# A two-part kernel on one core: the last output block turned, the first load and scan in two, and a new hand-written order

## The chip, the cores and the metric

One core of one Trainium2 chip runs the whole program. The metric is the device time of one execution in microseconds; the kernel before has a median of 391.71 us over three executions (391.2 to 394.22). The engines have names of their own in the rows: PE is TensorE's multiplication and PEld its weight load, DVE is VectorE, ACT is ScalarE, POOL is GpSimd, SP is SyncE (here the engine that issues nearly all transfers).

## The reference

A linear attention with decays (4 batches, 8 heads, 768 steps, head size 48) feeds a small network with a maximum of three products:

```python
for t in range(S):
    cur = einsum('bhd,bhe->bhde', u[None] * kt, vt)
    y[:, :, t] = einsum('bhd,bhde->bhe', rt, state + cur)
    state = wt[:, :, :, None] * state + einsum('bhd,bhe->bhde', kt, vt)
x = y.transpose(0, 2, 1, 3).reshape(3072, 384)
h = maximum(maximum(x @ w1, x @ w2), x @ w3)      # 3072 x 768
out = (h @ w_out).astype(float32)                 # 3072 x 384
```

The weights of the network arrive as 64-bit floats.

## The kernel before

**Attention.** The 768 steps are cut in 6 chunks of 128 for each of 4 batches, 24 pieces k = 0 to 23. A piece's decays `tin[.., 0:517]` hold four blocks of 129 columns with a zero at each block's border, so that one scan serves four pairs of heads. Its steps have one letter each: `b` the backward scan of the decays (line 406), `p` the floor of four end values (415), `q` their reciprocal (418), `f` the forward scan (421), `r` decays times receptance and key (430), `d`, `e` the diagonal (443 on ScalarE, then 460 on TensorE and 463 on VectorE), `X` the scores (489), `M` their mask (496 on VectorE, 500 on ScalarE), `T` a transposition (511, copied by 513), `R`, `U`, `S`, `m`, `Z` the state, `V` and `Y` the values (593 or 614, with a tiny ScalarE copy "touch" between the two at 598 or 620), `E` the result into `x`, `n` the next load (271), `c3` and the like a check on ScalarE (435).

**The network.** Tokens come in 6 halves of 512 (`HT`). For each half 18 groups (`up`, line 175) make the three products for six blocks of 128 hidden units, ScalarE and VectorE take their maximum out of PSUM (158, 160), and `downs` (211) multiplies with `w_out`. Values and weights are split in a high and a low part, three products each; the first four blocks of the first half use plain 32-bit products. For halves 0 to 4 the result is turned (`across`): three tiles of 128 outputs x 512 tokens, 54 products of 512 columns. For the last half it is natural: four tiles of 128 tokens x 384 outputs, 72 products of 384 columns.

**Weights.** They are loaded (`w`, line 329) and turned to 32 bits: `l` on ScalarE (346, 347), `h` and `c` on VectorE (352, 358), `s` and `o` split them (140, 141).

**Order.** Every engine works through its own instructions in the order in which the program is written, and the order is set by hand: `PARTS` is a list of steps through the first two halves (453 of them, about the first 165 us), and after it a loop takes a fixed mix of attention units and groups. `g..` and `G..` are groups of the first and second half, `D..` and `H..` pieces of `downs`, `t` takes one product out of PSUM. `W10` puts ten products of a tile of zeros into TensorE's queue, `warmer(WARM, LEAD)` the first ones and `warmer(0, BACK)` some after the last product.

**The end.** A flag computed on the way tells whether the fast path's assumptions held. Each engine reads it (line 820) and branches (821) over a slow second path. The last two of the four natural tiles stay in PSUM over that branch (`LATE = 2`); behind it ScalarE copies one and VectorE the other, and SyncE stores each (932, 933).

## Time and profile before

| | |
|---|---|
| three executions | 391.2, 391.71, 394.22 us |
| the profiled execution | 391.18 us, of it 389.5 us span |
| PE busy | 381.7 us (98%) |
| DVE busy | 265.9 us (68%) |
| ACT busy | 173.4 us (45%) |
| POOL busy | 85.2 us (22%) |
| TensorE's granted clock, mean | 0.998 of 2.4 GHz |

The span goes from the first to the last instruction; 1.7 us of the execution lie around it. A product's end is modelled in these records, so a busy PE may still be waiting; how fast it really goes is seen from the starts of products that follow each other.

### The profile page before, as it was taken

What the parts mean: (1) busy time and instruction counts of PE and PEld (TensorE: products, weight loads), DVE (VectorE), ACT (ScalarE), POOL (GpSimd) and SP (SyncE); (2) the same over time, 40 slices, a digit from 0 to 9 for tenths busy, and PEclk for the clock granted to TensorE, in tenths of its full rate; (3) what the DMA queues carried; (4) which work ended last, traced back from release to release, by engine and by line L of the source; (5) the groups of instructions that cost most, each with busy time, mean ns of one, the idle gap of its engine ahead of it and who ended that gap; (6) DMA issues with size and microseconds to landing.
All of it is one profiled execution on the core that took longest, in us unless ns stands there. A gap on an engine that the chain in (4) does not pass through costs nothing.

```text
span 389.5 us, 10503 instructions
## 1 busy us (share of the span) xinstructions
PE 381.7 (98%) x4480; PEld 309.3 (79%) x4480; DVE 265.9 (68%) x399; ACT 173.4 (45%) x373; POOL 85.2 (22%) x102
## 2 busy tenths in 40 slices
PE   8899999999999999999999999999999999999995
PEld 4688867766788888888888888888888887878895
DVE  7999999986779975598778567777568431432320
ACT  4688787643544443333444443443443332421210
POOL 3000000221443252144424314333414100000000
PEclk9999999999999999999999999999999999999999
DMA  7993897301823431477243866143951123200002
GB/s 284 403 347 103 284 406 248 112 2 52 272 68 126 147 127 51 136 292 223 68 173 115 275 198 210 61 168 98 307 201 44 42 82 89 94 3 1 0 24 67
DMA packets 23576, 58.44 MB, mean 150 GB/s; under 512 B 2720, under 2 KB 3712, under 8 KB 23520
## 3 DMA queue, kind: packets, MB, share of 16 engines
q1 hardware_dynamic: 20144, 48.58, 36.0%
q10 hardware_dynamic: 3376, 9.09, 7.3%
q8 instruction: 37, 0.61, 0.6%
q14 instruction: 19, 0.16, 0.1%
HBM read 51.87 MB, written 4.72 MB: 145 GB/s over the span
## 4 chain that ended last, share of the span: by engine, by line
PE 86%; DVE 6%; DMA 3%; ACT 2%; issue 2%; SPq 0%; POOL 0%; ACTq 0%; DVEq 0%
PE psm L175 53%; PE psm L211 18%; PE grams L489 3%; PE y L527 3%; PE y L614 3%; DMA w<-in_w_all_dram 2%; PE psm L511 2%; PE grams L542 1%; DVE w L358 1%; PE grams L460 1%; DVE cv L352 1%; PE grams L211 1%; PE y L211 1%; DMA tin<-in_tin_dram 1%; DVE w L141 1%
## 5 line engine op out<-in xcount | busy, mean ns | idle before, releaser
L175 PE MATMUL psm<-x_hi,w 128*128 128x512 f32 x576 | 183.0, 393 | 0.0
L175 PEld LDWEIGHTS psm<-x_hi,w 128*128 128x128 f32 x576 | 108.1, 188 | 23.5 <-issue 0.2
L175 PE MATMUL psm<-x_lo,w 128*128 128x512 f32 x288 | 112.1, 389 | 0.0
L160 DVE TENSOR_TENSOR m<-psm,m 128x512 f32<-128x512 f32 x64 | 43.7, 685 | 51.2 <-PE psm L175 44.2
L175 PEld LDWEIGHTS psm<-x_lo,w 128*128 128x128 f32 x288 | 54.1, 188 | 11.1 <-issue 0.2
L211 PE MATMUL psm<-h_hi,w 128*128 128x512 f32 x180 | 59.5, 430 | 0.3 <-DVE h_hi L160 0.3
L140 ACT CAST h_hi<-m 128x512 fp32r<-128x512 f32 x32 | 19.6, 617 | 54.6 <-DVE m L160 54.6
L211 PEld LDWEIGHTS psm<-h_hi,w 128*128 128x128 f32 x180 | 33.4, 188 | 12.1 <-issue 4.8
L470 POOL TENSOR_SCALAR_AFFINE_SELECT a<-sums 64x512 f32<-64x512 f32 x32 | 25.2, 787 | 72.3 <-DVE sums L467 71.3
L435 ACT ACTIVATE gf<-gf 112x1034 f32<-112x1034 f32 x24 | 25.7, 1070 | 26.4 <-DVE tin L430 26.2
L415 POOL TENSOR_SCALAR d_fwd<-gf 112x4 f32<-112x4 f32 x24 | 6.6, 276 | 134.6 <-DVE gf L406 128.3
L421 DVE TENSOR_TENSOR_SCAN gf<-tin,d_fwd 112x517 f32<-112x517 f32 x24 | 35.6, 1482 | 0.4
L406 DVE TENSOR_TENSOR_SCAN gf<-tin,d_bwd 112x517 f32<-112x517 f32 x24 | 30.2, 1258 | 5.7 <-DMA tin<-in_tin_dram 5.6
L175 PE MATMUL psm<-x,w 128*128 128x256 f32 (+1 forms) x126 | 33.9, 418 | 0.0
L430 DVE TENSOR_TENSOR tin<-tin,gf 112x1024 f32<-112x1024 f32 x24 | 31.1, 1296 | 0.0
L211 PE MATMUL psm<-h_lo,w 128*128 128x512 f32 x78 | 30.4, 390 | 0.0
L141 DVE TENSOR_TENSOR h_lo<-m,h_hi 128x512 fp32r<-128x512 f32 x32 | 23.9, 752 | 7.7 <-ACT h_hi L140 7.5
L175 PEld LDWEIGHTS psm<-x,w 128*128 128x128 f32 x126 | 23.0, 190 | 6.8 <-issue 3.3
L447 POOL TENSOR_TENSOR kr<-kr,u_bc 128x384 f32<-128x384 f32 x16 | 27.7, 1730 | 1.3
L141 DVE TENSOR_TENSOR x_lo<-x,x_hi 128x512 fp32r<-128x512 f32 x18 | 11.4, 685 | 22.7 <-ACT x_hi L140 22.7
L446 POOL TENSOR_TENSOR kr<-kr 128x384 f32<-128x384 f32 x16 | 22.9, 1434 | 9.4 <-DMA kr<-in_nat_dram 8.4
L382 ACT ACTIVATE cv<-cv,mid_top 128x384 f32<-128x384 uint32 x24 | 14.9, 621 | 16.6 <-DVE cv L380 16.5
(99 smaller groups left out, 468.6 us busy)
## 6 DMA issues: line engine op xcount, KB each, us to landing
tin<-in_tin_dram SPq DMA_DIRECT2D x24, 512.0 KB, 4.5
w<-in_w_all_dram SPq DMA_DIRECT2D x25, 384.0 KB, 7.6
w<-in_w_all_dram ACTq DMA_DIRECT2D x23, 384.0 KB, 3.4
v<-in_nat_dram SPq DMA_DIRECT2D x24, 288.0 KB, 5.4
tin<-in_tin_dram SPq DMA_DIRECT2D x24, 262.5 KB, 5.3
kr<-in_nat_dram SPq DMA_DIRECT2D x16, 384.0 KB, 5.1
out_dram<-m SPq DMA_DIRECT2D x15, 256.0 KB, 2.5
x<-x SPq DMA_DIRECT2D x10, 96.0 KB, 2.9
```

What stands on the lines that cost most here:

```text
L140: nc.scalar.copy(out=hi, in_=src)
L141: rest = lambda: nc.vector.tensor_tensor(out=lo, in0=src, in1=hi.bitcast(F32), op=ALU.subtract)
L160: nc.vector.tensor_tensor(out=m[:, cols], in0=ps[:, cols], in1=m[:, cols], op=ALU.max)
L175: nc.tensor.matmul(ps[:, cols], lhsT=wt[i][:, ct * 128:(ct + 1) * 128], rhs=x[part][:, ct, cols], start=(n == 0), stop=(n == KT * len(term ...
L211: nc.tensor.matmul(pss[tt][:, 0:wide_to], lhsT=w[:, cut] if turned else h[:, cut], rhs=h[:, :] if turned else w[:, :], start=(f == 0 and i ...
L406: nc.vector.tensor_tensor_scan(out=g[0:112, ::-1], data0=t[0:112, 0:WC][:, ::-1], data1=d_bwd[0:112, ::-1], initial=0.0, op0=ALU.mult, op1 ...
L421: nc.vector.tensor_tensor_scan(out=prep[k]["f"][0:112, :], data0=tbuf[k % NB][0:112, 0:WC], data1=d_fwd[0:112, :], initial=0.0, op0=ALU.mu ...
L430: nc.vector.tensor_tensor(out=both[0:112], in0=both[0:112], in1=by[0:112], op=ALU.mult)
L435: nc.scalar.activation(out=flat, in_=flat, func=AF.Square, accum_out=acc[0:112, k:k + 1])
L446: nc.gpsimd.tensor_tensor(out=n[:, 0, :], in0=n[:, 0, :], in1=n[:, 1, :], op=ALU.mult)
L447: nc.gpsimd.tensor_tensor(out=n[:, 0, :], in0=n[:, 0, :], in1=u_bc[:, :], op=ALU.mult)
L470: nc.gpsimd.affine_select(out=a[o:o + HC, 0:H, :], in_=cs[o:o + HC, :].unsqueeze(2).broadcast_to([HC, H, HC]), pattern=[[0, H], [1, HC]], ...
```

## The change

The last half is turned as the others: `natural` goes, `downs` has one form, and one tile (`LATE = KT - 1`, 128 x 512) stays in PSUM over the branch. Behind it VectorE copies its first 256 columns and ScalarE the others, and one transfer stores both. The first piece's decays load in two transfers, cut at column 259 (`CUT`), and their backward scan runs as two; their floor moves from GpSimd to VectorE. `PARTS` has the same steps in another order (`W9`, `W4`, `W5` for `W10`, `W3`, `W3`), and three numbers change.

```diff
-WARM = 9
-LEAD = 69
-BACK = 8
+WARM = 8
+LEAD = 86
+BACK = 5
...
-PARTS = """b0 w w p0 q0 f0 d0 b1 e0 p1 q1 R0 w d1 r0 W10 X0 c0 w T0 f1 W3 M0 b2 n3 p2 e1 r1 V0 q2 U0 W3 d2 l w X1 f2 w Y0 E0 M1
+PARTS = """w b0 d0 p0 q0 f0 b1 w R0 e0 p1 q1 W9 r0 w X0 d1 f1 c0 M0 W4 b2 T0 n3 e1 p2 l w W5 q2 r1 d2 f2 V0 X1 c1 M1 T1 h
...
-LATE = 2
+LATE = KT - 1
 LINE = 128
+CUT = NP // 2 * WS + 1
...
         def load(k):
...
-            for cols in (slice(0, WU), slice(RK, TU)):
+            for cols in (*((slice(0, CUT), slice(CUT, WU)) if k == 0 else (slice(0, WU),)), slice(RK, TU)):
                 nc.sync.dma_start(out=t[:, cols], in_=tin[b, c, :, cols])
...
-            nc.vector.tensor_tensor_scan(out=g[0:112, ::-1], data0=t[0:112, 0:WC][:, ::-1],
-                                         data1=d_bwd[0:112, ::-1], initial=0.0, op0=ALU.mult, op1=ALU.add)
+            for cut in (slice(0, CUT), slice(CUT, WC)) if k == 0 else (slice(0, WC),):
+                nc.vector.tensor_tensor_scan(out=g[0:112, cut][:, ::-1], data0=t[0:112, cut][:, ::-1],
+                                             data1=d_bwd[0:112, cut][:, ::-1], initial=0.0, op0=ALU.mult, op1=ALU.add)
...
-            nc.gpsimd.tensor_scalar(out=sep, in0=prep[k]["g"][0:112, 1:WC:WS], scalar1=FLOOR, scalar2=None, op0=ALU.max)
+            eng = nc.gpsimd if k else nc.vector
+            eng.tensor_scalar(out=sep, in0=prep[k]["g"][0:112, 1:WC:WS], scalar1=FLOOR, scalar2=None, op0=ALU.max)
...
-                    nc.tensor.matmul(pss[tt][:, 0:wide_to], lhsT=w[:, cut] if turned else h[:, cut],
-                                     rhs=h[:, :] if turned else w[:, :],
+                    nc.tensor.matmul(pss[tt][:, :], lhsT=wt[FT * 3 + f][:, cut], rhs=ht[f][:, :],
...
-        while groups < GPH * NH - DPH + 2 * CPH:
+        while groups < GPH * NH:
...
-    last = w_p.tile([128, 2, 2 * PC], F32, name=f"w{spot}")
-    for tt in range(LATE, CPH):
-        o = last[:, tt - LATE, 0:PC]
-        (nc.scalar.copy if tt < CPH - 1 else nc.vector.tensor_copy)(out=o, in_=left[tt][:, 0:DM])
-        nc.sync.dma_start(out=natural[tt], in_=o)
+    last = w_p.tile([128, 2, 2 * PC], F32, name=f"w{spot}")[:, 0, 0:HT]
+    nc.vector.tensor_copy(out=last[:, 0:HT // 2], in_=left[:, 0:HT // 2])
+    nc.scalar.copy(out=last[:, HT // 2:], in_=left[:, HT // 2:])
+    nc.sync.dma_start(out=across[NH - 1, LATE], in_=last)
```

The order at three places, first of before and then of the change. SyncE, from the program's first transfer (`tin` decays and keys, `v` and `x` values, `w` weights):

```order
L271 DMA tin_107<-in_tin_dram 128x525
L271 DMA tin_107<-in_tin_dram 128x1024
L271 DMA tin_108<-in_tin_dram 128x525
L271 DMA tin_108<-in_tin_dram 128x1024
L261 DMA v<-in_nat_dram 128x576
L265 DMA x<-in_nat_dram 128x384
L271 DMA tin_109<-in_tin_dram 128x525
L271 DMA tin_109<-in_tin_dram 128x1024
L329 DMA w_242<-in_w_all_dram 128x1536 x2
L261 DMA v<-in_nat_dram 128x576
L265 DMA x<-in_nat_dram 128x384
L329 DMA w_279<-in_w_all_dram 128x1536 x2
```

```order
L268 DMA tin_107<-in_tin_dram 128x259
L268 DMA tin_107<-in_tin_dram 128x266
L268 DMA tin_107<-in_tin_dram 128x1024
L268 DMA tin_108<-in_tin_dram 128x525
L268 DMA tin_108<-in_tin_dram 128x1024
L258 DMA v<-in_nat_dram 128x576
L262 DMA x<-in_nat_dram 128x384
L268 DMA tin_109<-in_tin_dram 128x525
L268 DMA tin_109<-in_tin_dram 128x1024
L326 DMA w_257<-in_w_all_dram 128x1536 x2
L258 DMA v<-in_nat_dram 128x576
L262 DMA x<-in_nat_dram 128x384
```

The first transfer became two, and every later one stands one place further back.

ScalarE, eleven rows from the check of piece 0 (`gf,sums`) on; `kr<-tin_109` is step `d` of piece 2, `cv<-w` and `w<-w` the first weight pair's step `l`, `touch` and `x<-y` belong to the values of the first pieces:

```order
L435 ACTIVATE gf,sums<-gf 112x1034
L513 COPY kn<-psm 128x448
L500 COPY a_137<-grams 128x256
L598 COPY touch<-y 112x2
L443 ACTIVATE kr<-tin_109 112x128 x4
L346 ACTIVATE cv<-w_242,low_end 128x768
L347 ACTIVATE w_242<-w_242 128x768
L632 COPY x<-y 128x3x128
L500 COPY a_138<-grams 128x256
L513 COPY kn<-psm 128x448
L598 COPY touch<-y 112x2
```

```order
L434 ACTIVATE gf,sums<-gf 112x1034
L499 COPY a_138<-grams 128x256
L512 COPY kn<-psm 128x448
L343 ACTIVATE cv<-w_257,low_end 128x768
L344 ACTIVATE w_257<-w_257 128x768
L442 ACTIVATE kr<-tin_109 112x128 x4
L597 COPY touch<-y 112x2
L434 ACTIVATE gf,sums<-gf 112x1034
L499 COPY a_139<-grams 128x256
L512 COPY kn<-psm 128x448
L631 COPY x<-y 128x3x128
```

The first weight pair's two rows moved ahead of the diagonal of piece 2 and of the first `touch`.

The engines behind the branch, with what a row waits for; VectorE's row and then ScalarE's, the last rows of each before the program's end (`PE_49`, `DVE_49` and `Activation_49` are the counts of the three engines' finished instructions, `DMAHW` those of transfers):

```order
L821 UNCONDITIONAL_BRANCH
L821 UNCONDITIONAL_BRANCH [waits DVE_49]
L932 COPY w_6175<-grams 128x384 [waits DVE_49,PE_49]
L997 UNCONDITIONAL_BRANCH
L821 UNCONDITIONAL_BRANCH
L821 UNCONDITIONAL_BRANCH [waits Activation_49]
L932 COPY w_6175<-y 128x384 [waits DMAHW4_49,DVE_49,PE_49]
L997 UNCONDITIONAL_BRANCH
```

```order
L818 UNCONDITIONAL_BRANCH
L818 UNCONDITIONAL_BRANCH [waits DVE_49]
L923 COPY w_5843<-grams 128x256 [waits DVE_49,PE_49]
L989 UNCONDITIONAL_BRANCH
L818 UNCONDITIONAL_BRANCH
L818 UNCONDITIONAL_BRANCH [waits Activation_49]
L924 COPY w_5843<-grams 128x256 [waits DMAHW5_49,DVE_49]
L989 UNCONDITIONAL_BRANCH
```

In ScalarE's row the wait for TensorE's count is gone, and VectorE's count and a transfer's are left; VectorE's row waits for TensorE in both.

## Rows read from the trace of the kernel before

**Rows 1.** Page, parts 1 (busy us, share, instructions) and 4 (chain)
```profile
PE 381.7 (98%) x4480; PEld 309.3 (79%) x4480; DVE 265.9 (68%) x399; ACT 173.4 (45%) x373; POOL 85.2 (22%) x102
...
PE 86%; DVE 6%; DMA 3%; ACT 2%; issue 2%; SPq 0%; POOL 0%; ACTq 0%; DVEq 0%
```

**Rows 2.** Chain of waits: start us, us, what, count; four stretches
```profile
147.81 12.46 PE psm L211 x54
...
372.58 6.26 PE psm L211 x36
...
381.97 3.14 PE grams L211 x18
385.13 0.56 DVE w L932
```

**Rows 3.** Timeline, first 10 us: start, us, engine line operation, count, [idle before <-releaser]
```profile
0.81 1.81 SPq L271 DMA_DIRECT2D tin<-in_tin_dram  x4
...
3.56 1.23 DVE L406 TENSOR_TENSOR_SCAN gf<-tin,d_bwd 112x517 f32<-112x517 f32 x1 [1.11 <-DMA tin<-in_tin_dram]
...
4.88 0.23 POOL L415 TENSOR_SCALAR d_fwd<-gf 112x4 f32<-112x4 f32 x1 [1.24 <-DVE gf L406]
...
5.07 1.28 ACT L443 ACTIVATE kr<-tin 112x128 f32<-112x128 f32 x4 [2.76 <-DMA tin<-in_tin_dram]
...
5.36 1.24 DVE L421 TENSOR_TENSOR_SCAN gf<-tin,d_fwd 112x517 f32<-112x517 f32 x1
...
7.64 0.70 DVE L463 COPY_PREDICATED a<-mask,grams 128x512 f32<-128x512 int32 x1
...
8.31 1.20 DVE L430 TENSOR_TENSOR tin<-tin,gf 112x1024 f32<-112x1024 f32 x1
...
9.56 0.90 PE L489 MATMUL grams<-tin 48*64 48x128 f32 x32 [0.31 <-DVE tin L430]
```

**Rows 4.** Timeline of TensorE, 17 to 22 us
```profile
17.13 0.69 PE L460 MATMUL grams<-tin,kr 48*64 48x64 f32 x32 [0.31 <-ACT a L500]
...
20.55 0.90 PE L489 MATMUL grams<-tin 48*64 48x128 f32 x32
...
21.82 1.47 PE L175 MATMUL psm<-x,w 128*128 128x256 f32 x6
```

**Rows 5.** Timelines of ScalarE and VectorE, a row of each
```profile
14.54 1.02 ACT L346 ACTIVATE cv<-w,low_end 128x768 uint32<-128x768 uint16 x1
...
18.58 1.21 DVE L430 TENSOR_TENSOR tin<-tin,gf 112x1024 f32<-112x1024 f32 x1
```

**Rows 6.** Timeline of TensorE, 72 to 88 us: its two longest waits
```profile
72.23 0.69 PE L460 MATMUL grams<-tin,kr 48*64 48x64 f32 x32 [0.55 <-DVE scur L563]
...
85.66 2.46 PE L211 MATMUL psm<-h_hi,w 128*128 128x512 f32 x6 [0.26 <-DVE h_hi L160]
```

**Rows 7.** Timeline of SyncE's issues after 376 us
```profile
376.84 2.93 SPq L765 DMA_DIRECT2D out_dram<-m  x2
384.07 1.98 SPq L933 DMA_DIRECT2D out_dram<-w  x2
```

**Rows 8.** Timeline of ScalarE after 376 us
```profile
378.94 0.48 ACT L216 COPY m<-psm 128x384 f32<-128x384 f32 x1 [2.12 <-PE psm L211]
382.49 0.48 ACT L932 COPY w<-y 128x384 f32<-128x384 f32 x1 [3.07 <-ACTq L821]
```

**Rows 9.** Groups by form, 0 to 170 us: count | busy us, mean ns
```profile
L160 DVE TENSOR_TENSOR h_hi<-psm,h_hi 128x256 f32<-128x256 f32 x12 | 5.0, 413 | 0.4 <-ACT h_hi L158 0.2 <-PE psm L175 0.2
...
L158 ACT COPY h_hi<-psm 128x256 f32<-128x256 f32 x6 | 2.2, 374 | 1.0 <-PE psm L175 1.0
```

**Rows 10.** Page, part 6: DMA issues, KB each, median us to landing
```profile
out_dram<-m SPq DMA_DIRECT2D x15, 256.0 KB, 2.5
```

**Rows 11.** Line 821, the branch: duration ns min/median/max, first and last start
```profile
L821 SPq EVENT_SEMAPHORE  x8: 17/17/17, 383.3 to 383.9; - x8
...
L821 PEldq COMPARE_BRANCH  x1: 4034/4034/4034, 383.8 to 383.8; - x1
```

More of the change, by code (lines that the diff above doesn't have):

```diff
@@ L142, in split, with moe @@
         rest() if later is None else later.append(rest)
-    def moe(x, pools, store, late=None, plain=0, turned=True):
+    def moe(x, pools, store, late=None, plain=0):
         ps_m, hp, mp = pools
@@ L155, in take_up @@
             m = top[f]
-            n = taken[f, cols.start] = taken.get((f, cols.start), 0) + 1
+            n = taken.get((f, cols.start), 0) + 1
+            for at in range(cols.start, cols.stop, C):
+                assert taken.get((f, at), 0) == n - 1
+                taken[f, at] = n
             if n == 1:
@@ L199, in downs @@
         def downs():
-            order = [(tt, f) for tt in range(KT if turned else CPH) for f in range(FT)]
+            order = [(tt, f) for tt in range(KT) for f in range(FT)]
             order.insert(FT, order.pop(FT - 1))
-            wide_to = HT if turned else DM
             pss = {}
@@ L764, in store @@
             def store(tt, o):
-                nc.sync.dma_start(out=natural[tt] if half == NH - 1 else across[half, tt], in_=o)
-            up, catch_up, ups, down = moe(xs[half], pools, store, late if half == NH - 1 else None, plain=FR if half == 0 else 0,
-                                          turned=half < NH - 1)
+                nc.sync.dma_start(out=across[half, tt], in_=o)
+            up, catch_up, ups, down = moe(xs[half], pools, store, late if half == NH - 1 else None, plain=FR if half == 0 else 0)
             now = dict(half=half, up=up, catch_up=catch_up, ups=ups(), down=down())
@@ L801 @@
         groups = 2 * GPH
-        while groups < GPH * NH - DPH + 2 * CPH:
-            half = min(groups // GPH, NH - 1)
-            g = groups - half * GPH
+        while groups < GPH * NH:
+            half, g = divmod(groups, GPH)
             if g == 0:
@@ L903 @@
         yt = ytr.rearrange("k p b (h t) -> k p b h t", t=C)
-        def again_moe(half, of, turned):
+        with tc.For_i(0, NH) as half:
             x = xs_p.tile([128, KT, HT], F32, name="x")
@@ L914, in store2 @@
             def store2(tt, o):
[L915 to L917 removed]
+                nc.sync.dma_start(out=across[ds(half, 1), tt].rearrange("h p t -> (h p) t"), in_=o)
+            _, _, ups, down = moe(dict(hi=x_hi, lo=x_lo), pools, store2)
             for part in (ups, down):
```

54 lines of the change are left out of this document (21 added, 33 removed).

## The prediction

> **What bounds the kernel now.** First the page's busy times and chain: PE is busy for 381.7 of 389.5 us and makes 86% of the chain [rows 1]. Then, because a busy PE may still be waiting, the stretches of the chain in order of time: 54 products of 512 columns take 12.46 us, 231 ns each, and the last part's 72 products of 384 columns run from 372.58 to 385.11 without a hole (the first 36 and the last 18 stand there), 12.53 us or 174 ns each [rows 2]. From about 20 us on the products follow each other at this pace, so the reader should see two ends and little between them: about 20 us before TensorE has steady work, and 4.4 us behind its last product. Whatever reaches the end must change what TensorE waits for in those first 20 us, its few later waits, or the tail.
>
> The start is a chain of transfer, VectorE, TensorE: the first decays are issued at 0.81, the scan starts at 3.56, GpSimd's floor at 4.88, the forward scan at 5.36, `r` ends at 9.51 and the first scores start at 9.56 [rows 3]. VectorE stands still for almost nothing between 5.36 and 9.51. The first product with weights starts at 21.82, behind the scores of piece 2 at 20.55 [rows 4]. Later the two longest waits of TensorE are 0.55 us at 72.23, for VectorE's state row, and the one ending at 85.66, for a `take_up` of VectorE's [rows 6].
>
> **The change part by part.** I sum against the profiled execution's own 391.18 us; the median of the three, 391.71, lies 0.5 above it.
>
> *The split load and scan, the floor.* Four issues on SyncE take 1.81 us, 0.45 each [rows 3]. The first half's landing has no row. It comes no later than the whole did (scan at 3.56), and with half the bytes I give it 0.3 us, to 3.25; the bound on the other side is 2.9, where a transfer of 2 us or so would put it. A half scan costs between half of 1.23 us and that plus a smallest operation's 0.2: 0.66. The second half is issued 0.45 later and lands inside that time. So the scans end at 4.57, not 4.79. The floor took GpSimd 0.23 us plus two changes of engine, from 4.79 to the reciprocal, which with its own 0.2 leads to 5.36; on VectorE the same four columns cost some 0.1 to 0.2, which saves 0.2. The forward scan starts at 4.95, 0.4 earlier. But the extra issue puts every later transfer back by up to 0.45: the keys of piece 0, for which ScalarE waits until 5.07, land at 5.5, `d` takes 1.28, and TensorE's diagonal and VectorE's copy (7.64) follow it, now at 7.5 [rows 3]. VectorE runs in order, so `r` behind that copy gains only what the copy gains. The first scores start at 9.4, not 9.56. Bounds: 0.6 us gained if the later transfers are held up by nothing but the shared bandwidth, 0.45 lost if they shift whole and the first half lands no sooner.
>
> The Trainium skill's page "VectorE: DVE Perf Modes", section on the TRN2 errata, says that an operation on SBUF pays a fixed latency once per instruction, so that two small ones pay it twice; its 58 to 150 cycles would be an estimated 0.06 to 0.16 us for the second scan. My 0.66 for a half (0.62 is exact half) holds 0.04 of it; by the page the gain here is up to 0.1 us smaller.
>
> *The new order up to the first weight product.* Two things move. VectorE now does `b3`, 1.2 us, before the diagonal and `r` of piece 2; ScalarE does the first weights' `l` before `d2` and the first touch, where before `l` began at 14.54 [rows 5]. `l` cannot start before both weights have landed, and `d2` and the touch are queued behind it; TensorE's `Y0` waits for the touch and its diagonal of piece 2 for `d2`. Before, ScalarE had no idle time ahead of `l` at 14.54, so the weights had landed by then; with 1.9 us for `l` and 1.3 for `d2` the touch comes near 16.2 if they land at 12.9, and TensorE's diagonal of piece 2 at about 17.6, against 17.13 [rows 4]. VectorE's copy and `r2` then end near 20.05, and the scores of piece 2 start at 20.1 against 20.55, because between the two TensorE has only 1.65 us of other work. The first weight product, whose weights VectorE joins behind `r2`, starts at about 21.4 against 21.82. I take **-0.4 us** up to here; the ends are -0.8 and +1.2, the second if the weights land as late as 14.5.
>
> *The order from there to 165 us.* The steps are the same 453, so TensorE's work is the same but for filler in its queue: 26 products of zeros for 25, under the waits of the first 15 us. A shift can come from waits alone. Both long waits of rows 6 lose their cause: the diagonal `e7` now stands 20 steps behind `S6` instead of 9, which releases its accumulator, and the last plain group (`gc3`) no longer stands just ahead of the first piece of `downs` but three groups earlier. The rows show 0.8 us of waiting; as a product's end is modelled late, the true holes are longer, and I count 1.3. A new order has waits of its own that no row shows; with nothing between 0 and as many again plus a slow stretch (+3), I take +1.0. Together **-0.3**, from -1.3 to +1.7. Cover: `r2` ends at 19.79 [rows 5] and its scores start at 20.55, so VectorE may be 0.8 us late there before it is felt.
>
> *The last half.* 54 products at 231 ns are 12.46 us, 72 at 174 ns were 12.53 [rows 2]: **-0.07**. The columns are the same, 27,648.
>
> *The tail.* Let C be the start of VectorE's last copy, 385.13. Before, that copy took 0.56 [rows 2] and the last store was issued at C + 0.56. Now two things stand there. First, ScalarE's copy no longer waits for TensorE's count but for VectorE's; since it reads what TensorE writes, that can only be the count of VectorE's own last copy, which waits for TensorE. So the two halves run one after the other: 0.41, then 0.37 for 256 columns [rows 9], with a change of engine C + 0.9. Second, SyncE: from the end of its last ordinary store, 379.77, to its first issue behind the branch, 384.07, it needs 4.30 us [rows 7], though the copy it then stores had ended at 382.97 [rows 8] and its eight waits at the branch lie at 383.3 to 383.9 [rows 11]. It was 1.6 us early for the last store; now only one tile of 18 products, 4.16 us, stands behind the last ordinary store instead of two (6.27). ScalarE's copy of that tile starts at C - 4.1, takes 0.59 by the two widths in rows 8 and 9, the issue ends at C - 3.15, and SyncE is ready at C + 1.15. The last store goes out 0.6 us later than before. Its 256 KB land in 2.5 us [rows 10], as before. **+0.6**, between +0.35 (the copies alone) and +0.8. ScalarE's own 3.07 us over the branch [rows 8] end at C - 0.4, just hidden; TensorE's branch ends at 387.9 [rows 11], ahead of the landing in both.
>
> Sum: -0.4 - 0.3 - 0.07 + 0.6 = -0.2, so 391.0 us.
>
> **The rivals.** (a) *The start gains nothing.* The first half lands no earlier than the whole did, later loads shift, and the tail's loss stands alone: 391.18 + 0.6 - 0.07 + 0 = 391.7, or 391.4 with the -0.3. For it: ScalarE and VectorE both wait for transfers in the first 5 us [rows 3], and there the issue is the pace. Against it: the floor saves 0.2 in any case. The skill's page "DMA: Bandwidth & Descriptors", section on the anatomy of one DMA, speaks for this one: most of a transfer's time is its completion, not its bytes, and its 436 GB/s would make 130 KB less worth an estimated 0.3 us, so its figure agrees with mine while its rule warns against more; the 2.75 us from issue to scan are in line with it.
>
> (b) *The first weights hold up ScalarE* (slower). `l` stands ahead of `d2` and the touch. Each 0.1 us that the second weight lands after 12.9 goes to TensorE's diagonal and the scores of piece 2, and from there to the end, since TensorE has no holes to take it up. The point from which it decides is a landing at about 13.3; at 14.5 the loss is 1.2 instead of a gain of 0.4: 391.2 + 1.2 - 0.3 - 0.07 + 0.6 = 392.6. To lose over 1% (395.6) it would take a further 3 us of waits later, the end of my range for the new order.
>
> (c) *All waits vanish.* The start gains 0.8, the known waits 1.3, the tail costs 0.35: 391.18 - 0.8 - 1.3 - 0.07 + 0.35 = 389.4. Against it: 453 steps in another order hardly have no wait anywhere.
>
> (d) The last half's turning saves more than its columns say, by fewer weight loads: the 72 products were paced at 174 ns for 160 ns of columns at 2.4 GHz, the 54 at 231 for 213, an overhead of 14 and 18 ns; there is nothing to win, and it goes with my forecast.
>
> **How the numbers follow.** The forecast, 389.9 to 391.9, has 0.55; (a) 0.16; (b) 0.20, of which 0.03 lie above 395; (c) 0.09, of which 0.02 below 388. The range, 389.4 to 393.0, leaves out about 2 in 10 of (b) and the outer parts of (c) and of the forecast's own error. A measurement of this kernel tells about 1% from no change: faster by over 1% is below 387.8, slower above 395.6. That gives 0.02, 0.95 and 0.03.
>
> **What would show it.** The first scan row should be two of about 0.66 us, the first from 3.25 on; the floor a VectorE row; the first scores at 9.4 and the first weight product at 21.4. ScalarE's idle time before its first `l` row decides between forecast and (b). There should be no wait over 0.5 us at `e7` or the first `downs`. The last ScalarE copy should start where VectorE's ends, and the last store be issued about 1.15 us after C with the span ending 0.6 us later behind the last product than before. I am wrong if TensorE has new waits of several microseconds between 22 and 165 us, or if the two halves of the last copy overlap.

## The result, and the profile after

The changed kernel takes 394.06 us, median of 22 executions (392.52 to 399.59), against 391.39 (389.78 to 394.22) for the kernel before on the same chip: 2.7 us slower, ratio 1.0075, 95% interval [1.0061, 1.0089]. The ratio, here and below, is taken over fast executions alone (it leaves out the one of 399.59 us) and is not the quotient of the medians. The time is within 1% of before, where the forecast put 0.95 of its chance, but above its range (389.4 to 393.0). The profiled execution spans 393.0 us, 389.5 before.

Busy times and the chain on the page of the profile after, to be read beside [rows 1]:

```profile
PE 382.5 (97%) x4477; PEld 307.7 (78%) x4477; DVE 267.4 (68%) x401; ACT 172.5 (44%) x373; POOL 85.1 (22%) x101
...
PE 90%; DMA 3%; DVE 2%; ACT 2%; issue 1%; POOL 1%; SPq 0%; ACTq 0%; DVEq 0%; POOLq 0%
```

TensorE does the same work in a longer span: it stands still for 10.5 us instead of 7.8, in waits or at the two ends. The start, against [rows 3] (timeline of SyncE's issues, VectorE and ScalarE):

```profile
0.81 2.29 SPq L268 DMA_DIRECT2D tin<-in_tin_dram  x5
3.04 1.28 DVE L404 TENSOR_TENSOR_SCAN gf<-tin,d_bwd 112x259 f32<-112x259 f32 x2 [0.59 <-DMA tin<-in_tin_dram]
4.36 0.17 DVE L414 TENSOR_SCALAR d_fwd<-gf 112x4 f32<-112x4 f32 x1
4.78 1.24 DVE L420 TENSOR_TENSOR_SCAN gf<-tin,d_fwd 112x517 f32<-112x517 f32 x1
6.27 1.28 ACT L442 ACTIVATE kr<-tin 112x128 f32<-112x128 f32 x4 [3.97 <-DMA tin<-in_tin_dram]
...
10.04 0.67 PE L488 MATMUL grams<-tin 48*64 48x128 f32 x21
```

The forward scan is 0.6 us earlier, but the keys reach ScalarE 1.2 us later and the first scores 0.5 us later (10.04, 9.56 before). Next the first weights and what stands behind them on ScalarE, against [rows 4, 5] (timelines of ScalarE and of TensorE):

```profile
14.19 1.02 ACT L343 ACTIVATE cv<-w,low_end 128x768 uint32<-128x768 uint16 x1 [1.33 <-DMA w<-in_w_all_dram]
17.08 0.16 ACT L597 COPY touch<-y 112x2 f32<-112x2 f32 x1
17.29 0.45 PE L592 MATMUL y<-a,v 64*64 64x128 f32 x8 [0.85 <-ACT touch L597]
...
23.01 1.35 PE L177 MATMUL psm<-x,w 128*128 128x256 f32 x5
```

ScalarE waits 1.33 us for the weights, the touch ends at 17.24, TensorE waits for it, and the first weight product starts at 23.01 instead of 21.82. Both waits of [rows 6] are gone. In their place stands the longest wait of the trace. First SyncE's issues and what waits for the keys and values `kr` of piece 10 (timeline), then the end of that chain, then TensorE's row with its idle time (timeline):

```profile
104.51 4.60 SPq L268 DMA_DIRECT2D tin<-in_tin_dram  x2
109.21 1.42 SPq L255 DMA_DIRECT2D kr<-in_nat_dram  x1
114.76 1.02 POOL L445 TENSOR_TENSOR kr<-kr 128x384 f32<-128x384 f32 x1 [4.31 <-DMA kr<-in_nat_dram]
116.91 0.56 DVE L466 TENSOR_REDUCE sums<-kr 128x8 f32<-128x384 f32 x1 [3.98 <-POOL kr L446]
```

```profile
121.00 1.86 DVE gf L420
122.86 0.02 issue
122.88 1.24 DVE tin L429
124.12 0.04 issue
124.16 0.60 PE psm L510 x4
```

```profile
124.16 0.60 PE L510 MATMUL psm<-ident,tin 112*128 112x112 f32 x4 [1.33 <-DVE tin L429]
```

SyncE stands 4.60 us in the issue of piece 11's decays, whose buffer is not free; the keys of piece 10 are queued behind it. VectorE stands 3.98 us in the middle of its queue, works off what has piled up, and finishes `r` so late that TensorE starts its next products 1.5 us late, at 124.16. (The row says 1.33 us idle; since a product's end is modelled late, waits near 122 us are counted below by the pace of the products, which makes each 0.2 longer.) The end, against [rows 2, 7, 8, 10, 11] (chain of waits, timeline, the store's landing, and the branch's row):

```profile
374.70 8.16 PE psm L211 x36
382.86 4.09 PE grams L211 x18
```

```profile
386.97 0.42 DVE L923 COPY w<-grams 128x256 f32<-128x256 f32 x1 [10.17 <-PE grams L211]
387.43 0.37 ACT L924 COPY w<-grams 128x256 f32<-128x256 f32 x1 [3.89 <-DVE w L923]
388.34 0.35 SPq L925 DMA_DIRECT2D out_dram<-w  x1
```

```profile
out_dram<-w SPq DMA_DIRECT2D x1, 256.0 KB, 3.4
```

```profile
L818 PEldq COMPARE_BRANCH  x1: 3817/3817/3817, 384.4 to 384.4; - x1
```

The last part starts 2.1 us late (374.53 by the first product, 372.42 before) and takes 12.25 us (12.53). From VectorE's last copy, C, to the end of the span pass 6.01 us, 4.33 before. The store goes out at C + 1.37 and lands 3.4 us later, not 2.5.

### The profile page after: what moved, and what is told of

The parts are those of the page before. It is cut to its first block, busy times and chain, and to the rows that moved or that the text cites. A ratio compares the mean times of both kernels' runs of the same rounds, so it can differ in the third digit from the quotient of the medians.

```text
span 393.0 us, 10494 instructions
## 1 busy us (share of the span) xinstructions
PE 382.5 (97%) x4477; PEld 307.7 (78%) x4477; DVE 267.4 (68%) x401; ACT 172.5 (44%) x373; POOL 85.1 (22%) x101
## 3 DMA queue, kind: packets, MB, share of 16 engines
HBM read 51.87 MB, written 4.72 MB: 144 GB/s over the span
## 4 chain that ended last, share of the span: by engine, by line
PE 90%; DMA 3%; DVE 2%; ACT 2%; issue 1%; POOL 1%; SPq 0%; ACTq 0%; DVEq 0%; POOLq 0%
PE psm L177 55%; PE psm L211 19%; PE y L526 3%; PE y L613 3%; PE grams L488 3%; PE psm L659 2%; PE psm L510 2%; DMA w<-in_w_all_dram 2%; DMA kr<-in_nat_dram 1%; PE grams L541 1%; PE grams L211 1%; PE grams L459 1%; DVE tin L429 1%; ACT kr L442 1%; PE psm L657 1%
## 5 line engine op out<-in xcount | busy, mean ns | idle before, releaser
L211 PE MATMUL psm<-h_hi,w 128*128 128x512 f32 x204 | 66.7, 425 | 0.0
L211 PEld LDWEIGHTS psm<-h_hi,w 128*128 128x128 f32 x204 | 37.9, 188 | 12.5 <-issue 5.3
L469 POOL TENSOR_SCALAR_AFFINE_SELECT a<-sums 64x512 f32<-64x512 f32 x32 | 26.7, 833 | 71.1 <-DVE sums L466 66.6
L420 DVE TENSOR_TENSOR_SCAN gf<-tin,d_fwd 112x517 f32<-112x517 f32 x24 | 37.9, 1578 | 0.3
L434 ACT ACTIVATE gf<-gf 112x1034 f32<-112x1034 f32 x24 | 25.7, 1072 | 25.4 <-DVE tin L429 25.4
L211 PE MATMUL psm<-h_lo,w 128*128 128x512 f32 x90 | 35.1, 390 | 0.0
L404 DVE TENSOR_TENSOR_SCAN gf<-tin,d_bwd 112x517 f32<-112x517 f32 (+2 forms) x25 | 29.6, 1187 | 3.6 <-ACT gf L434 2.0
L140 DVE TENSOR_TENSOR h_lo<-m,h_hi 128x512 fp32r<-128x512 f32 x32 | 22.5, 709 | 8.4 <-ACT h_hi L139 8.2
L512 ACT COPY kn<-psm 128x448 f32<-128x448 f32 x20 | 10.7, 535 | 31.6 <-PE psm L510 31.6
L445 POOL TENSOR_TENSOR kr<-kr 128x384 f32<-128x384 f32 x16 | 20.9, 1306 | 9.9 <-DMA kr<-in_nat_dram 5.1
```

Of the source, the lines that this page charges most:

```text
L140: rest = lambda: nc.vector.tensor_tensor(out=lo, in0=src, in1=hi.bitcast(F32), op=ALU.subtract)
L211: nc.tensor.matmul(pss[tt][:, :], lhsT=wt[FT * 3 + f][:, cut], rhs=ht[f][:, :], start=(f == 0 and i == 0), stop=(f == FT - 1 and i == len( ...
L404: nc.vector.tensor_tensor_scan(out=g[0:112, cut][:, ::-1], data0=t[0:112, cut][:, ::-1], data1=d_bwd[0:112, cut][:, ::-1], initial=0.0, op ...
L420: nc.vector.tensor_tensor_scan(out=prep[k]["f"][0:112, :], data0=tbuf[k % NB][0:112, 0:WC], data1=d_fwd[0:112, :], initial=0.0, op0=ALU.mu ...
L434: nc.scalar.activation(out=flat, in_=flat, func=AF.Square, accum_out=acc[0:112, k:k + 1])
L445: nc.gpsimd.tensor_tensor(out=n[:, 0, :], in0=n[:, 0, :], in1=n[:, 1, :], op=ALU.mult)
```

## The experiments

Differences below 0.5 us between medians of different chips say little: the kernel before measured 390.67 beside back14, act_store, kr_first and l_later, and 391.1 to 391.4 beside the others. Two theories were set against each other first: **O**, the new order has waits of its own; **T**, the tail costs most of it. The table gives for each profile the time from the first scores to the last part, which takes the start's scatter out; C to the end of the span; how far the last of the last store's 16 completions lies behind the fifteenth; and over all executions the median less that of the kernel before on the same chip, with the ratio. A median and a ratio can differ by up to 0.8 us where a kernel's executions fall in two groups.

| kernel | scores to last part | C to end | 16th behind 15th | median, us | ratio, 95% |
|---|---|---|---|---|---|
| before | 362.86 | 4.33 | 0.63 | | |
| the change | 364.50 | 6.01 | 1.36 | +2.7 | 1.0075 [1.0061, 1.0089] |
| order_alone | 363.09 | 3.70 | 0.01 | +2.0 | 1.0037 [1.0008, 1.0066] |
| order_back | 362.53 | 6.96 | 2.37 | +2.5 | 1.0044 [1.0023, 1.0065] |
| tail_alone | 362.68 | 4.84 | 0.35 | +0.8 | 1.0017 [0.9997, 1.0036] |
| split_alone | 362.75 | 4.23 | 0.61 | +0.5 | 1.0031 [1.0001, 1.0061] |
| back14 | 362.74 | 4.61 | 0.15 | +2.9 | 1.0067 [1.0041, 1.0093] |
| act_store | 362.94 | 6.08 | 1.65 | +3.0 | 1.0092 [1.0058, 1.0126] |
| kr_first | 364.81 | 6.57 | 2.18 | +4.3 | 1.0098 [1.0074, 1.0122] |
| l_later | 362.14 | 6.13 | 1.72 | +3.2 | 1.0078 [1.0060, 1.0096] |
| kr10_first | 362.17 | 6.81 | 2.38 | +1.7 | 1.0053 [1.0039, 1.0066] |
| no_fill | 366.20 | 6.31 | 1.86 | +5.0 | 1.0143 [1.0125, 1.0161] |
| turned_fixed | 362.40 | 4.41 | 0.01 | +0.2 | 1.0017 [1.0003, 1.0032] |
| order_fixed | 362.80 | 3.89 | 0.19 | -0.5 | 0.9990 [0.9979, 1.0000] |
| before_back1 | 362.64 | 6.13 | 2.44 | -0.2 | 0.9999 [0.9976, 1.0021] |
| order_fixed2 | 362.61 | 4.22 | 0.53 | +0.3 | 1.0003 [0.9984, 1.0021] |
| order_fixed2_split | 363.31 | 4.49 | 0.87 | +0.4 | 1.0004 [0.9984, 1.0023] |
| order_back_back14 | 363.32 | 4.59 | 0.01 | +0.6 | 1.0029 [1.0011, 1.0047] |
| kr10_back14 | 362.48 | 4.72 | 0.32 | +0.2 | 1.0006 [0.9993, 1.0019] |
| order_fixed_back14 | 362.08 | 4.67 | 0.96 | +0.2 | 1.0002 [0.9990, 1.0014] |

**The change taken apart.** order_alone is the kernel before with the new `PARTS`, `WARM`, `LEAD` and `BACK`; order_back the change with the old ones; tail_alone the kernel before with the turned last half alone; split_alone with the split load and scan and VectorE's floor alone.

> The kernel before with nothing but the new step order and its three filler numbers: one load, one scan, floor on GpSimd, natural last half. Theory O (the order is what costs the 2.1 us that stand ahead of the last part): the first product of the group that ended the changed kernel's long stretch is again about 2 us late, VectorE's last copy starts near 387.1 instead of 385.1, TensorE waits over 1 us near 122 us for r, and the time is 2.0 us above before (ratio 1.005). Rival S (the split load is what delays the keys and the first weights, and the order only shows it): the first weight product comes within 0.3 us of 21.8, the wait near 122 stays, so at most 0.8 us (ratio 1.002). Rival N: the order costs nothing by itself, ratio 1.000.

> The changed kernel with the old step order and the old filler numbers: split load and scan, floor on VectorE and turned last half stay. Theory O: the two microseconds ahead of the last part are gone, the tail's 1.7 us stay, the 54 turned products give 0.25 back, and the split gives nothing: before + 1.4 us (ratio 1.0036). Theory S: the first weights land late here too, the last copy starts 1 us later than before's 385.1, and the time is before + 2.5 (ratio 1.0065). If the split's gain of 0.6 us at the forward scan reaches the end: before + 0.8 (ratio 1.002).

> The kernel before with nothing but the turned last half: 54 products, one tile kept over the branch, its copy cut between VectorE and ScalarE, one store. Everything up to 372 us is as before. Theory T (the tail costs 1.7 us: copies one after the other, SyncE ready 0.8 us later, the landing 0.9 us longer): before + 1.45 us (ratio 1.0037), 6.0 us from VectorE's last copy to the end of the span. My forecast's tail (+0.6, landing 2.5 us): before + 0.5 (ratio 1.0013) and 4.9 us. If the longer landing hangs on the eight instead of five filler products behind the last real one, it lies in between, with a landing other than 3.4 us.

> The kernel before with nothing but the split load and scan of the first decays and the floor on VectorE. Theory: the forward scan starts 0.6 us earlier (4.8 instead of 5.36), but each later load is issued 0.46 us later and the keys of piece 0 reach ScalarE about 1.2 us later (6.3 instead of 5.07), so that the first scores start 0.5 us later and the first weight product up to 0.5 us later: before + 0.4 us (ratio 1.001). Rival 1 (the 0.6 us count): before - 0.5 (ratio 0.9987). Rival 2 (work of the first 20 us takes it up): ratio 1.000 within 0.0005.

The parts do not add up to 2.7 us in a simple way. order_alone has the wait near 122 us (0.94 us) but not the one near 32, and its last copy starts at 386.20, not 387.1. order_back has no new wait ahead of the last part, and yet the worst tail. tail_alone has the tail I had forecast: its store goes out at C + 1.17 and lands in 2.4 us. So one and the same last half ended 4.84 or 6.96 us behind C, and little but the landing differs. The medians of order_alone and split_alone are mixtures: six of order_alone's twelve executions have a mean granted clock of 0.991 to 0.995 and spans of 391.7 to 393.2 us, the other six 0.998 or more and 388.5 to 390.9; in split_alone four at 0.991 span 392.9 to 393.5, the other eight 389.2 to 391.5. Both profiles are of the shorter kind, so no trace shows what most of order_alone's +2.0 is. The landing of order_back's last store (view of the transfers in the tail):

```profile
out_dram<-w SPq DMA_DIRECT2D x1, 256.0 KB, 4.4
```

What the landings meet stands in the trace's packets. In the change's tail, the transfers of two stretches, 388.95 to 389.10 and 390.05 to 391.5 us:

```profile
q8 instruction: 1, 0.02, 54.0%
...
q1 hardware_dynamic: 9, 0.02, 4.6%
```

One instruction packet of 16 KB starts at 389.00 and lasts 1.295 us; the store's packets on 15 of the 16 DMA engines are through at 390.0; on one engine eight packets of 2 KB and the completion start at 390.28, where the instruction packet ends, and end at 391.29. (The rows do not name a packet's DMA engine; that it is one and the same is read from these times.) In order_back it lies from 387.60 to 389.45 and that engine's eight packets end at 390.43; in tail_alone it starts at 388.77, behind the store's last packet. The packet comes 0.7 us behind the end of TensorE's branch (388.26 in the change, 386.86 in order_back; [rows 11] before), in some profiles up to 1.8 us, and no row shows why. Theory **L**: instruction fetch and last store meet on one DMA engine, and which stands first there decides 1 to 2.4 us. The number that sets it is `BACK`: fewer products behind the last real one let TensorE reach its branch earlier. With 8 of them and the turned form it can go either way: the branch ended 1.68 us behind C in tail_alone and 1.69 in order_back, and the store went out at C + 1.17 and C + 1.31.

Each branch of TensorE brings two packets of 16 KB, the other one 1.0 us or more behind the branch's start. That one meets the first of the two last stores in the kernel before: it lies from 384.82 to 386.39, eight packets of that store start at 386.37, and its last completion comes at 387.75, 1.8 us behind the fifteenth; the last store's, queued behind them, comes 0.63 late. So 4.33 us is not an undisturbed tail: the natural form takes 3.7 where the last store's completions come together (order_alone), the turned one 4.4 (turned_fixed).

**The tail.** The three edits below are, in this order, those of back14 (order_back_back14 is order_back with 14 in place of its 8), of act_store, and of before_back1, which is the kernel before, natural last half and all, with an earlier branch.

```diff
-BACK = 5
+BACK = 14
```

```diff
-    nc.sync.dma_start(out=across[NH - 1, LATE], in_=last)
+    nc.scalar.dma_start(out=across[NH - 1, LATE], in_=last)
```

```diff
-BACK = 8
+BACK = 1
```

> The changed kernel with 14 instead of 5 small products of zeros behind its last real product; nothing else moves. Theory L (the last store's landing is long because a 16 KB instruction fetch, which comes 0.7 us behind the end of TensorE's branch, stands ahead of the store's packets on one of the 16 DMA engines): nine more products let TensorE reach its branch some 1.5 us later, the fetch starts 3.3 us or more behind the start of VectorE's last copy instead of 2.0, behind the store's packets, the last of the 16 completions comes within 0.5 us of the others instead of 1.36, and the time from VectorE's last copy to the span's end falls from 6.0 to 5.0 us: ratio 1.005 instead of 1.0075. Rival P (a store of 256 KB whose packets are 2 KB simply lands in 3.4 us): 6.0 us stays. Rival B (TensorE's branch becomes the end): 6.0 or more.

> The changed kernel with its last store issued by ScalarE, behind its own copy, instead of by SyncE. Theory L with SyncE late: ScalarE's copy ends 0.83 us behind the start of VectorE's, so the store goes out at 0.85 instead of 1.37 and its packets are through before the fetch, which stays at 2.0: landing 2.5 instead of 3.4, together 1.4 us less, 4.6 us from VectorE's last copy to the end: ratio 1.004 instead of 1.0075. If only SyncE's lateness counted (landing stays 3.4): 5.5 us, ratio 1.006. If ScalarE's own issue path is as late as SyncE's: 6.0, ratio 1.0075.

> The kernel before with one product of zeros behind its last real product instead of eight; nothing else moves. Theory L (the instruction fetch behind TensorE's branch delays the last store where the two meet on one DMA engine, whatever the form of the last half): TensorE reaches its branch 1.2 us earlier, so the fetch starts 1.6 to 2.2 us behind the start of VectorE's last copy instead of 3.4, in the middle of the last store's packets; the last of its 16 completions comes 1 us or more behind the others, 5.0 to 6.5 us pass from VectorE's last copy to the end instead of 4.3, and the ratio is 1.0015 to 1.005. Rival P (the turned tile's store lands late by its own form): 4.3 us and ratio 1.000.

> The changed kernel with the old order (as order_back) and 14 products behind the last real one instead of 8. Theory L: order_back's trace had the last of the 16 completions 2.4 us behind the others and 6.95 us from VectorE's last copy to the end; here the fetch starts at least 3 us behind that copy, the landing is 2.4 us in all, 4.4 to 4.9 us pass to the end, and the ratio falls from 1.0044 to 1.000 to 1.002. Rival (the landing is late in the profiled executions alone, or for another reason): the ratio stays at 1.004.

The traces agree with L in each case. back14's store goes out at C + 1.17, its branch ends later, and the landing (view of the transfers) is

```profile
out_dram<-w SPq DMA_DIRECT2D x1, 256.0 KB, 2.2
```

act_store's (first line) comes from ScalarE at C + 1.12, 0.25 us earlier than the change's, and meets the fetch (packet at 387.02) all the same; before_back1 (second line, two stores of 192 KB), with the natural form, shows the same late completion as the turned ones:

```profile
out_dram<-w ACTq DMA_DIRECT2D x1, 256.0 KB, 3.7
```

```profile
out_dram<-w SPq DMA_DIRECT2D x1, 192.0 KB, 4.3
```

So the turned form is not the cause, and rival P, a store that simply lands that late, falls. The medians say less. before_back1's did not move: 8 of its 12 executions span 388.7 to 389.8 us, which leaves no room for the 1.8 us its profile lost, so the natural form met the fetch in a minority of them. order_back_back14 came down from +2.5 to +0.6 in the median, but by the ratio only from 1.0044 to 1.0029: two of its twelve executions span 392.5 and 392.8 us, ten 389.6 to 390.5. back14 did not come down in the median of six (spans 389.6, 389.7 and four from 391.6 to 393.0). Two of these four have a mean granted clock of 0.991 and 0.994, the other two 1.0 (391.6 and 392.2 us). What they met has no trace. With 14 the earlier one of the two packets comes close: in back14's profile it ends at 386.95 and the store's first packet starts at 387.11. That the two met in the longer executions is possible and not shown.

**The order.** kr_first moved `n10` behind `e8`, the wrong load: piece 9's keys were not the ones waited for. kr10_first puts `e9` (which issues piece 10's keys) ahead of `n11`. l_later puts the first weights' `l w` behind `V0`. order_fixed2 differs from order_fixed (below) in the third pair's `l`. The steps of `PARTS` that move, in this order:

```diff
-Z8 n10 r9 U8 D5 m8 e8 w x
+Z8 r9 U8 D5 m8 e8 n10 w x
...
-V8 t X9 U9 n11 e9 t d10
+V8 t X9 U9 e9 n11 t d10
...
-e1 p2 l w W5 q2 r1 d2 f2 V0 X1
+e1 p2 W5 q2 r1 d2 f2 V0 l w X1
...
-q3 l n5 R2 c V2 S2 w c2
+q3 n5 R2 c V2 S2 l w c2
```

> The changed kernel with the load n10 moved behind e8, so that SyncE issues the keys and values of piece 9 before the decays of piece 10, whose issue stands 4.6 us waiting for its buffer. Theory Q (that queueing is the wait of TensorE of 1.54 us at 122.6): the keys are issued near 104.6 instead of 109.2, GpSimd and VectorE have them 4 us earlier, the wait falls under 0.3 us, and the time by 1.3 us: ratio 1.004 instead of 1.0075. Rival V (VectorE's queue is late there anyway): the wait stays over 1 us, ratio 1.0075. Rival W (the 1.54 us come back as another wait before 160 us): as V, with the wait elsewhere.

> The changed kernel with step e9 moved ahead of n11, so that SyncE issues the keys and values of piece 10 ahead of the decays of piece 11, whose issue stands 4.6 us waiting for its buffer. (The run before that meant to do this moved piece 9's keys, which were not the ones that TensorE waited for.) Theory Q: GpSimd's product with these keys starts near 110 instead of 114.8 us, VectorE's sum behind it does not wait 4 us, and TensorE's wait near 122 us, 0.5 to 1.5 us in the kernels with this order so far, is under 0.3 us: before + 1.5 to 2 us (ratio 1.004 to 1.0055 instead of 1.0075). Rival V (VectorE is late there from its own queue): the wait stays at 0.4 us or more and the ratio at 1.0065 or more.

> The changed kernel with the first weight pair's ScalarE step moved behind the diagonal of piece 2 and the first touch, where the kernel before had it. Theory F (the first weights hold up ScalarE): the touch comes near 15.2 us instead of 17.1, TensorE's wait of 1.1 us at 16.2 goes, the scores of piece 2 come 0.9 us earlier relative to the first scores (11.5 us behind them now, 11.0 in the kernel before), and the time falls by 0.4 to 1.0 us: ratio 1.005 to 1.0065 instead of 1.0075. Rival G (the weights' step ends later and the first weight product waits for it): scores earlier, but the first weight product not, and no change of the time.

> The kernel order_fixed (natural last half, one load and scan, new order with two steps moved) with the third weight pair's ScalarE step moved behind the third touch and the state copy. Theory M (where these weights land late, as at 25.7 us in order_fixed's trace with 1.4 us of waiting, all of ScalarE's work behind them is late, and the first downs come 0.6 to 1 us later): the first downs start 73.1 to 73.5 us behind the first scores instead of 74.3, the last part 362.0 to 362.3 instead of 362.8, ratio 0.9975 to 0.9985. Rival (the delay is taken up by 165 us anyway): 362.8, ratio 0.999.

kr_first left its wait near 123 at 1.15 us. How long the wait is also varies by itself: back14, whose code is the change's up to the last product, has (timeline of TensorE)

```profile
122.35 0.60 PE L510 MATMUL psm<-ident,tin 112*128 112x112 f32 x4 [0.26 <-DVE tin L429]
```

and act_store, likewise, 0.59 us idle there, and their last parts come 362.74 and 362.94 us behind the first scores, the change's 364.50. So the 1.5 us are those of one execution. kr10_first removes the wait (timeline; SyncE, GpSimd, TensorE):

```profile
103.52 0.38 SPq L255 DMA_DIRECT2D kr<-in_nat_dram  x1
104.44 3.70 SPq L268 DMA_DIRECT2D tin<-in_tin_dram  x2
...
111.10 1.81 POOL L445 TENSOR_TENSOR kr<-kr 128x384 f32<-128x384 f32 x1
...
121.79 0.60 PE L510 MATMUL psm<-ident,tin 112*128 112x112 f32 x4
```

The keys are issued ahead of the decays, GpSimd has them 3.7 us earlier and no longer waits; the last part comes 362.17 us behind the first scores. In the median 1.0 us is gained, over five executions. l_later's ScalarE has the touch ahead of the weights and does not wait for them (timeline of ScalarE):

```profile
14.68 0.16 ACT L597 COPY touch<-y 112x2 f32<-112x2 f32 x1 [0.83 <-PE y L592]
14.75 1.03 ACT L343 ACTIVATE cv<-w,low_end 128x768 uint32<-128x768 uint16 x1
```

The scores of piece 2 come 10.84 us behind the first (11.50 in the change, 10.99 before), and the last part is as early as in kr10_first, but the median gains nothing. The change's third wait, 0.74 us idle at 32.78, stands in kr_first and order_fixed too (0.62 and 0.72); in these three the third weight pair kept ScalarE waiting 0.84 to 1.43 us at 25.7 to 26.0. It is not the weights alone, for in order_fixed2, where that step is moved, TensorE still waits 0.63 us there; and the move gained nothing.

**Together.** turned_fixed is the change with kr10_first's, l_later's and back14's edits; kr10_back14 leaves out l_later's; order_fixed is the kernel before (natural, one load, `BACK = 8`) with the new order and the edits of kr10_first and l_later; order_fixed_back14 has `BACK = 14`; order_fixed2_split adds the split load to order_fixed2.

> The changed kernel with three mends at once: the first weight pair's ScalarE step behind the diagonal of piece 2 and the first touch, e9 ahead of n11, and 14 products behind the last real one, so that the instruction fetch comes behind the last store's packets. Theory (these three hold all that the change cost but the tail's serial copies and the late SyncE, +0.3 to 0.6 us): last part 362.1 us behind the first scores, landing 2.4 us, 4.6 us from VectorE's last copy to the end, time equal to before within 0.5 us (ratio 0.9985 to 1.001). Rival (a cause that these do not touch): ratio over 1.003.

> The kernel turned_fixed with the first weight pair's ScalarE step put back where the change had it, ahead of the diagonal of piece 2 and the first touch. Rival (b) of the prediction as it was put (each 0.1 us that the weights hold up ScalarE goes to the end): turned_fixed + 0.6 to 0.8 us, ratio 1.0035. Theory R (VectorE and ScalarE make the delay good before 147 us, as the last part came 362.2 us behind the first scores both in kr10_first and in l_later): turned_fixed within 0.3 us, ratio 1.001 to 1.0025.

> The kernel before (one load, one scan, floor on GpSimd, natural last half, 8 products behind the last) with the new order and two of its steps moved: the first weight pair's ScalarE step behind the diagonal of piece 2 and the first touch, and e9 ahead of n11. Theory O' (the new order is worth something once these two are mended, since its two old waits are gone): the last part starts 362.2 us behind the first scores instead of 362.9, no wait of TensorE over 0.5 us between 20 and 165 us, and the time is before - 0.3 to - 0.6 us (ratio 0.9985 to 0.999). Rival (the order costs by something else that no row has shown, or the clock of TensorE falls more often with it, as with order_alone): ratio 1.003 or more, with a mean granted clock of 0.991 to 0.995 in about half of the executions.

> The kernel order_fixed (natural last half, one load, new order with two steps moved, ratio 0.999 over its runs) with 14 instead of 8 products behind the last real one, so that the fetch behind TensorE's branch comes later than the last store's packets in every execution. Theory: ratio 0.998 to 0.9995, with fewer executions over 390.5 us of span. Rival (TensorE's own branch, now 1 us later, becomes the end, or the collision hardly occurs in the natural form): 0.999 to 1.001.

> The kernel order_fixed2 with the first decays' load and scan in two and the first floor on VectorE, as in the change. Theory X (in the mean of the traces so far the first scores start at 9.9 with the split and at 10.2 us without it, since the copy that precedes them follows TensorE's products and not the keys alone): 0.2 to 0.4 us less than order_fixed2, ratio 0.9965 to 0.998. Rival Y (the keys and weights that land later by 0.5 us or more eat it): ratio as order_fixed2 or 0.001 higher.

kr10_back14 brings the two causes together. With two small edits, one pair of steps exchanged and nine more products of zeros, the change is level with the kernel before: 1.0006 [0.9993, 1.0019]. Against kr10_first (1.0053 [1.0039, 1.0066]), from which only `BACK` differs, that is 1.8 us for the fetch and the store (1.5 by the medians); against the change, kr10_first's exchange is 0.9 us, by ratios whose intervals overlap a little. The first weights still hold up ScalarE there (1.13 us at 14.36), and turned_fixed, without that, is no faster: theory R, by which VectorE and ScalarE make the delay good before 147 us. order_fixed is 0.1% under the kernel before in eleven executions, order_fixed_back14 level with it in twelve: no version is measurably faster than before. order_fixed_back14's last completion, 0.96 us behind the others, is a meeting too, with the earlier packet: that lies from 386.04 to 387.38, and the late engine's eight packets start at 387.36. So 14 products keep the later packet off the last store and can bring the earlier one onto it. The split load made no difference that these runs can tell.

**The clock.** no_fill is the change without `W9`, `W4` and `W5`.

> The changed kernel without the 18 products of zeros that W9, W4 and W5 put into TensorE's queue in the first 15 us; nothing else moves. Theory K (the executions of 3 us more, at a mean granted clock near 0.991 instead of 0.998, are those in which TensorE's clock falls to 1.2 GHz in the sparse first 20 us, and the products of zeros hold it up): every execution has a mean clock of 0.992 or less, the trace shows the clock at half of full speed for some 3 to 10 us between 10 and 30 us, and the time is 2 to 4 us above the changed kernel's (ratio 1.012 to 1.018). Rival (the zeros only fill idle time): clock and time as the changed kernel's, ratio 1.0075.

TensorE's busy time, granted clock and the transfers in four stretches of no_fill (columns: stretch, its length, PE busy, clock, DMA share, GB/s):

```profile
0.00:10.20 10.20, 7.05 (x153) 1.00 0.82 287
10.20:23.90 13.70, 12.38 (x236) 0.50 0.78 289
23.90:40.00 16.10, 16.10 (x320) 1.00 0.88 326
```

Without the 18 products of zeros, which ran between 7.9 and 14.1 us in the change, the clock is at its lower level, 1.2 GHz, from 10.2 to 23.9 us. Before it falls, TensorE is busy for 0.41 of the 2 us from 8 to 10; before it rises, it has been busy without a hole since 18 us at the latest. The time is 2.3 us above the change's. One thing was not as expected: two of the four executions have a mean clock of 0.996 and 0.998 and are no shorter (spans 394.4 and 395.7). The clock's records begin with its first rise, 5.7 to 9.1 us into these profiles, so a late rise would not lower the mean; no profile shows that it was so.

## Why the prediction was wrong, point by point

- **The tail's landing (+0.6): the term mis-sized.** "Its 256 KB land in 2.5 us [rows 10], as before" failed: they landed in 3.4. The serial copies (0.42, then 0.37 us, [rows 9]) and SyncE's delay were right: the store at C + 1.13 to 1.17 in tail_alone, back14 and kr10_back14, at C + 1.37 in the change, forecast C + 1.15. Where the last store is not held up, C to the end is 4.4 to 4.8 us against 4.33, +0.1 to +0.5; against the 3.7 of a natural tail whose last store is not held up either it is +0.7 or more, near the forecast's +0.6. The kernel before, whose 4.33 I started from, is held up itself. I used TensorE's branch (387.9) as a possible end only and costed `BACK` 8 to 5 at nothing. Six of the seven profiles with the turned form, SyncE's store and a `BACK` of 5 or 8 show the late completion, none of the four with 14. The Trainium skill's page "Runtime: NRT & Kernel Launch", section on instruction fetch, says that a taken branch whose target lies outside the window already loaded forces a fetch by DMA, in blocks of 16 KB, and counts it as a stall of the branching engine; the packet of that size is in the trace, but here it is another engine's store that pays. The Trainium skill's page "DMA: Bandwidth & Descriptors", section on queues and completion order, says that a DMA engine alternates between queues packet by packet, a packet being a group of descriptors; the eight rows of 2 KB that wait behind one of 16 KB are in line with it.
- **The new order (-0.3, to +1.7): the step "a new order has waits of its own" was right in kind, its size +1.0 too small, and I could have found the place.** I read SyncE's first rows and not the pair `n11 e9`, where a load that waits for its buffer stands ahead of one that is urgent; before, `e9` stood eight steps ahead of `n11`. The 0.9 us that the exchange gives back is no surer than the two ratios, whose intervals overlap. Both old waits vanished as forecast.
- **Rival (b) happened at its place and not in its effect.** The second weight landed at about 14.2, beyond the 13.3 from which it was to decide, ScalarE waited 1.1 to 1.8 us in every profile that keeps that order, and the first weight product came 1.2 us late. But "from there to the end, since TensorE has no holes to take it up" was wrong: kr10_back14 keeps this delay and is level with turned_fixed, and in the five profiles that have it and get the third pair in time the first `downs` come 73.4 to 73.7 us behind the first scores, 73.96 before: by 84 us VectorE and ScalarE had made it good.
- **The start (-0.4).** Half scans of 0.64 us (0.66 forecast), floor 0.17, forward scan at 4.78 (4.95): right. The first half's landing was worth more than the 0.3 us of the prediction, which came from the bytes alone: the scan starts at 3.07 us in the mean of thirteen profiles with the split and at 3.73 in seven without. The keys paid for it, 5.97 against 5.14 in the same means. In the change they came at 6.27, not 5.5, and the first scores at 10.04, not 9.4. The profile of before was an early one: the start with one load gave first scores at 9.56 to 10.57 in seven profiles, mean 10.04; with the split 9.60 to 10.41 in thirteen, mean 9.93. There was nothing to gain or lose.
- **The last half (-0.07)**: 12.25 against 12.53 us, -0.28: the 512-column products go at 227 ns each here, not at the 231 I took from an earlier stretch.
- **The sum.** Forecast: start -0.4, order -0.3, last half -0.07, tail +0.6. Measured: start about 0, order +0.9 (what the exchange of `n11` and `e9` gives back), last half -0.3, tail +0.1 to +0.5 without the fetch and 1.8 for it: +2.5 to +2.9, and the median moved by +2.7. The two large terms are differences between these same kernels, so that the sum meets the median says little by itself, and the parts do not simply add up: `BACK` alone (back14) brought the median nothing.

## What to carry to other kernels

Where the last store is issued close to a branch, look at when the engines' instruction fetches come, and let a store that ends the program either precede or follow them clearly; a filler count may be such a setting, and moving one fetch off a store can bring another onto it. When an order is changed, read each in-order queue at the places where it waits for a buffer, and see what urgent load stands behind. A forecast of a microsecond should not rest on the start of one profile when that start scatters by as much.

## What was not expected of the hardware

- A 16 KB instruction packet takes 0.92 to 1.85 us on its DMA engine in these tails, and the first three of the store's packets behind it about 230, 230 and 173 ns instead of 84; held up by the later one of the two packets, the store completes 1.4 to 2.4 us behind its other fifteen parts. Eight kernels have the natural tail, and in every one of them one of the two packets holds up one of the last two stores.
- In the kernels with the new order and `e9` behind `n11` (no_fill apart), 16 of 58 executions had a mean granted clock of 0.994 or less and took some 1 to 6 us more than the others; with `e9` ahead, none of 75. But the kernels with the old order show it as well: of the kernel before 4 of 127, of its variants and order_back's 9 of 60, four of them in split_alone. No profile caught one; in the profiles (no_fill apart) the clock's record stands at its lower level from 387.7 to 391.2 us on, behind the last product, and that alone makes the 0.995 of the change's profile. That the clock falls in the wait near 122 us is an inference that cannot be the whole of it, since the old order has no such wait. Where it falls stays open, and with it why the exchange of two steps and `BACK` gained 2.5 us together and `BACK` alone nothing in six executions.
